# Attention and gated projection on one core: transposes, tail scores and attention outputs share PSUM bank pairs by quarters, the gated tile is stored without padding, and the step order is written anew

## The chip, the cores and the metric

The kernel runs on one core of a Trainium2 chip. The metric is the device time of one execution in microseconds.

## The reference: what is computed

q, k and v are 8 batches x 8 heads x 576 rows x 64. Attention is causal by blocks of 64 rows. Its output, with the heads side by side, is the input x of a gated linear unit of width 512: a causal convolution over five rows gives the gate, x times w_val gives the value, and their product goes through w_out.

```
scores = scale * np.matmul(q, k.transpose(0, 1, 3, 2))
mask = block_i >= block_j                      # blocks of 64
attn = softmax(where(mask, scores, -1e9))
x = (attn @ v) with heads side by side         # 8 x 576 x 512
gate = 1 / (1 + np.exp(-gate_pre))             # gate_pre: conv of 5 taps over rows
out = gate * (x @ w_val) @ w_out               # 8 x 576 x 512, float32
```

## The kernel before, in words

**Work units.** A head pair p (0 to 31; batch p // 4) is the unit of attention on the first 512 rows of a batch. The last 64 rows of a batch (the tail) are handled for all eight heads together. The gated unit works on a ring of four batch slots, each 4 + 576 columns wide (`slot(b)`, line 219), cut into runs n of 464 columns (0 to 9, five to a ring, `RUN`).

**Steps.** The kernel has no loops over these units. The string PLAN (line 12) lists 987 steps as name/arguments/engine/banks, in the order in which they are emitted; each engine executes its own steps in that order, and semaphores tie the engines together. Engine letters are P (TensorE), V (VectorE, DVE in the profile), A (ScalarE, ACT), G (GpSimd, POOL) and S (the SP DMA queue). The steps used below:

- `lq`, `lk`, `lv`, `lt`, `lvt`, `lwv`, `lwo`, `lcv`: loads of q, k, v, the tails of q and k, the tail of v, w_val, w_out, the convolution weights. q and k land in five buffers, v in five, tails in two (lines 193 to 196).
- `cq`, `cv`, `ct`, `cvt`: casts to fp16. `ccv`, `cwv`, `cwo`: casts of the weights.
- `T` (16 transposes), `Te`: q and k of a pair transposed into a pair of PSUM banks, and the copy out. `TT`, `TTe`: the same for a batch's tails.
- `S/p.t` (t = 0, 1, 2), `E/p.t`: scores of 128 x 1024, and their exponentials on ACT (line 441). `SL`, `EL`: scores of the tail with itself.
- `mka`, `mkb`: zeros into the masked corners. `A` (20 matmuls of 65 columns), `N`: attention times v, and the division by the row sum (lines 490 and 491). `AT`, `NT` for the tail.
- `X`, `Xe` (line 229 or 231), `XT`, `XTe`: transposes into the ring `xt`.
- `C/n` (80 matmuls on 32 x 32 tiles), `CS/n.i`: convolution of a run into four banks, and tanh on ACT (line 598).
- `V/n.x` (4 matmuls of 464 columns), `Ve/n.x`: x times w_val, and gate times value into `gv` (line 613).
- `W`, `We`: w_out reordered. `O/u.t` (4 matmuls of 512 columns, 8 where t = 4), `Oe`, `Od`: 128 output rows of the batch pair u, copy out, store. `OL` is one half of the very last rows.

**PSUM.** There are eight banks. A step that writes two banks has the pair to itself from its first write until its copy-out has run: `where` (line 173) records the banks, `take` (line 175) hands them to the copy-out. The loop at the end (lines 667 to 690) frees steps on other banks from each other:

```
for x, at in held:
    if not at & mine:
        independent(i, x, overwrite)
```

so that what stays tied is what shares a bank: a writer waits for the copies out of its banks, and a copy-out waits for the latest writer of its banks. `T` uses half of each bank of its pair (2 x 512 fp16 values), `TT` and `X` a quarter (2 x 256 fp16), `SL` half (2 x 256 fp32), `A` 260 of 512 fp32 values.

**The gated tile.** `gv` has the ring's layout, with four unused columns per batch. A run of 464 columns is one `Ve`. `project` (line 618) takes 128 columns of `gv` at a time; the fifth block (t = 4) lies across two batches, so that it takes two groups of 64 columns and eight matmuls.

Of the kernel before, what the change touches and what calls it, by code (L numbers as in the profile page):

```python
# [12 lines left out]
lk/1/S ppool//G pdve//V lcv//S ccv//G CW//P/1 lq/1/A cq/1/V T/1/P/4+5 lq/0/S lk/0/S lt/0.1/S  # L13
lt/0.0/S ct/0/G lk/4/S lq/3/S CWe//V lk/3/S cq/3/G cq0/0/V T0/0/P/0+1 lq/2/S lk/2/S lq/4/S cq0/1/V
T0/1/P/2+3 Te/1/A pact//A S/1.1/P/4+5 lv/1.0/S lv/0.0/S lv/0.1/S S/1.0/P/6+7 lt/1.0/S lq/5/S
lv/2.1/S T0e/0/V lk/5/S T0e/1/A S/0.0/P/2+3 lv/1.1/S lv/2.0/S lvt/0/S lv/3.1/S lt/1.1/S TT/0/P/0+1
lk/6/S TTe/0/V lv/3.0/S lq/6/S cq/4/G E/1.1/A E/0.0/A lwv/1/S lwv/0/S SL/0/P/0+1 EL/0/A S/0.2/P/2+3
E/1.0/A S/1.2/P/4+5 E/1.2/A S/0.1/P/0+1 T/3/P/6+7 cq/2/V T/2/P/4+5 mka/1/G cv/0/G Te/3/A S/3.1/P/6+7
E/0.1/A T/4/P/0+1 Te/2/V S/2.2/P/4+5 lwo/1/S lwo/0/S E/0.2/A mka/0/G mkb/0/G lk/7/S S/2.1/P/2+3
lq/7/S lt/2.0/S Te/4/V S/4.0/P/0+1 E/3.1/A E/2.2/A E/2.1/A S/2.0/P/6+7 E/2.0/A A/0/P/4+5 S/3.2/P/6+7  # L20
cq/5/V T/5/P/2+3 lt/2.1/S lk/8/S lv/4.1/S lq/10/S E/4.0/A N/0/V cv/2/V X/0/P/4+5 mkb/1/G cv/1/G
A/1/P/0+1 lq/8/S Xe/0/V E/3.2/A S/4.1/P/4+5 N/1/V S/3.0/P/6+7 mkb/3/G mkb/2/G mka/2/G Te/5/A
S/5.0/P/2+3 lk/10/S E/4.1/A ct/1/G cv/3/G lv/4.0/S A/2/P/0+1 N/2/V lq/9/S lk/9/S lv/6.0/S E/3.0/A
mka/3/G S/5.1/P/4+5 E/5.1/A TT/1/P/6+7 TTe/1/V lv/5.1/S cvt/0/G cq/6/G A/3/P/0+1 N/3/V cwv/1/G
cwo/0/G E/5.0/A ct/2/G lv/7.1/S S/4.2/P/6+7 SL/1/P/4+5 lv/6.1/S EL/1/A mka/4/G cq/7/G E/4.2/A
mkb/4/G cq/8/G lq/13/S lv/5.0/S lv/7.0/S lvt/1/S lk/12/S lq/12/S lk/11/S lq/11/S AT/0/P/2 X/1/P/4+5
X/3/P/0+1 Xe/3/A T/6/P/6+7 Te/6/A X/2/P/0+1 Xe/2/A NT/0/V XT/0/P/3 S/6.0/P/6+7 E/6.0/A Xe/1/V
C/0/P/0+1+4+5 CS/0.1/A CS/0.0/A XTe/0/V cwv/0/V V/0.3/P/7 cwo/1/V Ve/0.3/V V/0.0/P/6 Ve/0.0/V
S/6.1/P/4+5 E/6.1/A W//P/0+1+2+3 We/0/A We/1/V S/5.2/P/6+7 TT/2/P/4+5 TTe/2/V V/0.2/P/2 SL/2/P/0+1
S/6.2/P/4+5 E/5.2/A T/7/P/6+7 Ve/0.2/V Te/7/V EL/2/A E/6.2/A V/0.1/P/0 S/7.0/P/4+5 mka/6/G E/7.0/A  # L30
S/7.1/P/2+3 T/8/P/6+7 Te/8/A E/7.1/A Ve/0.1/V O/0.0/P/4 Oe/0.0/V mkb/6/G S/8.1/P/6+7 E/8.1/A cq/10/G
T/10/P/0+1 Te/10/V S/7.2/P/4+5 cv/4/G A/4/P/2+3 S/8.0/P/6+7 N/4/V E/7.2/A E/8.0/A O/0.1/P/1 cq/9/G
cv/6/G T/9/P/2+3 Te/9/V O/0.2/P/0 Oe/0.2/V cv/7/G mka/7/G Oe/0.1/A mkb/7/G mkb/5/G mka/8/G
S/8.2/P/6+7 E/8.2/A A/6/P/4+5 N/6/V S/10.2/P/2+3 S/9.1/P/0+1 X/6/P/4+5 cv/5/V cvt/1/G mkb/8/G
mka/5/G lv/8.0/S lv/8.1/S E/9.1/A S/9.2/P/6+7 Xe/6/A A/7/P/0+1 lt/3.1/S lt/3.0/S E/9.2/A N/7/V
AT/1/P/5 E/10.2/A A/5/P/6+7 NT/1/V cq/12/G T/12/P/0+1 XT/1/P/5 X/7/P/2+3 N/5/V X/5/P/6+7 lq/14/S
lk/13/S lv/9.0/S lt/4.0/S lk/14/S lv/9.1/S lk/15/S lv/11.0/S lt/4.1/S lv/10.1/S XTe/1/V lq/15/S
cq/11/G lv/10.0/S lv/11.1/S lvt/2/S lv/12.1/S cv/8/G lv/13.1/S ct/3/G lv/12.0/S lk/16/S cq/13/G
lk/18/S Xe/7/V lq/18/S lq/16/S mkb/9/G w0/1.64.0/P/4 X/4/P/4+5 Te/12/A S/12.1/P/2+3 cq/14/G cv/9/G
lv/14.0/S lv/14.1/S Xe/5/A T/11/P/6+7 E/12.1/A Xe/4/V C/1/P/0+1+4+5 CS/1.1/A V/1.2/P/2 Te/11/V  # L40
CS/1.0/A S/10.1/P/6+7 Ve/1.2/V A/8/P/4+5 N/8/V E/10.1/A S/11.0/P/2+3 V/1.1/P/0 E/11.0/A S/10.0/P/4+5
# [70 lines left out]
def kernel(  # L112
# [44 lines left out]
    def one(b):  # L157
        return PS[0:128, b]
# [562 lines left out]
```

## Time and profile before

| what | us |
| --- | --- |
| median of three runs | 185.79 (185.62 to 188.61) |
| the profiled execution, its own time | 187.27 |
| its span, first to last instruction | 185.0 |
| PE busy | 162.9 (88%) |
| ACT busy | 144.3 (78%) |
| DVE busy | 115.5 (62%) |
| POOL busy | 81.6 (44%) |

The profile page gives busy time of each engine, a strip of 40 slices of the span, DMA queues, the chain of work that ended last, and groups of equal instructions. Other views used here are the timeline (instructions in order, with start and length; equal neighbours merged), the windows (busy time in chosen stretches) and the waits. A line number can be that of a helper: 136 is every matmul, 140 every transpose on TensorE, 229 and 231 every copy.

### The profile page before, as it was taken

To read this page: it belongs to the slowest core of one execution; us is meant where nothing else is said; L and a number is where in the kernel's file an instruction comes from. 1 tells how busy PE (TensorE), PEld (TensorE's weight loads), DVE (VectorE), ACT (ScalarE), POOL (GpSimd) and SP (SyncE) were. 2 spreads that over 40 slices of the span, in tenths; PEclk is the share of its full clock that TensorE was granted. 3 is DMA by queue.
4 is the path that set the end of the run, shared out by engine and by line. 5 is a ranking of instruction groups with operands and counts; after the bars stand their busy time and mean duration, and the time that the engine had idled before them with its cause. 6 is when DMAs were issued, how large, how long until landed. Compare 5 with 4: busy or idle time off the path is not lost.

```text
span 185.0 us, 8265 instructions
## 1 busy us (share of the span) xinstructions
PE 162.9 (88%) x3529; PEld 98.6 (53%) x3529; DVE 115.5 (62%) x218; ACT 144.3 (78%) x170; POOL 81.6 (44%) x197
## 2 busy tenths in 40 slices
PE   0658787779869999999999998999999999999992
PEld 0333574345754566756446564566556655665450
DVE  6725565758666887696486885578458765533730
ACT  2599999788868998989998879997796888362342
POOL 6226362564854787625550771862843306200000
PEclk9999999999999999999999999999999999999998
DMA  5896999987988899699598999994896634104076
GB/s 177 269 273 144 237 292 370 273 231 172 288 204 217 200 268 278 148 343 311 147 259 243 265 275 283 283 245 129 226 272 203 149 141 164 66 4 174 0 275 235
DMA packets 66494, 40.38 MB, mean 218 GB/s; under 512 B 40214, under 2 KB 60950, under 8 KB 66459
## 3 DMA queue, kind: packets, MB, share of 16 engines
q1 hardware_dynamic: 66042, 39.48, 75.3%
q8 instruction: 27, 0.44, 1.0%
q10 hardware_dynamic: 416, 0.39, 0.7%
q14 instruction: 9, 0.07, 0.1%
HBM read 30.42 MB, written 9.44 MB: 215 GB/s over the span
## 4 chain that ended last, share of the span: by engine, by line
PE 65%; DMA 11%; ACT 9%; DVE 6%; issue 3%; SPq 3%; POOL 1%; DVEq 0%; ACTq 0%; POOLq 0%
PE PS L136 59%; ACT pt L441 6%; DMA qks<-in_k_dram 6%; PE PS L140 5%; DMA qks<-in_q_dram 4%; DVE x L491 2%; DVE qkT L231 2%; SPq L243 2%; DMA vs<-in_v_dram 2%; ACT xt L229 1%; DVE gv L613 1%; DVE osb L231 1%; ACT osb L229 1%; POOL qk L231 1%; ACT qkT L229 1%
## 5 line engine op out<-in xcount | busy, mean ns | idle before, releaser
L441 ACT ACTIVATE pt<-PS 128x1024 f16<-128x1024 f32 x96 | 93.4, 1030 | 10.3 <-PE PS L136 8.4
L136 PE MATMUL PS<-xt,w_val 128*128 128x464 f16 x160 | 36.9, 360 | 0.3 <-ACT pt L456 0.2
L136 PE MATMUL PS<-qkT 64*128 64x256 f16 (+3 forms) x256 | 34.2, 319 | 2.5 <-ACT qkT L229 0.5
L136 PE MATMUL PS<-w_out,gv 128*128 128x512 f16 (+2 forms) x164 | 36.0, 376 | 0.2 <-DMA qks<-in_q_dram 0.2
L231 POOL CAST qk<-qks 128x1024 f16<-128x1024 f32 x28 | 29.1, 1042 | 15.2 <-DMA qks<-in_q_dram 4.1
L613 DVE SCALAR_TENSOR_TENSOR gv<-th,PS 128x464 f16<-128x464 f32 x40 | 24.8, 634 | 16.5 <-PE PS L136 10.0
L136 PE MATMUL PS<-v,pt 128*128 128x65 f16 (+1 forms) x896 | 31.5, 195 | 1.1 <-DVE x L491 0.3
L136 PEld LDWEIGHTS <-pt 128*128 128x128 f16 (+1 forms) x960 | 28.3, 103 | 6.9 <-issue 3.3
L136 PEld LDWEIGHTS <-qkT 64*128 64x128 f16 x512 | 16.7, 97 | 18.8 <-issue 11.8
L231 DVE COPY qkT<-PS 128x1024 f16<-128x1024 f16 (+1 forms) x19 | 22.6, 1192 | 3.6 <-PE PS L140 3.4
L598 ACT ACTIVATE th<-PS 128x928 f32<-128x928 f32 x20 | 17.8, 946 | 7.8 <-PE PS L136 7.7
L491 DVE TENSOR_TENSOR x<-PS,rc 128x512 f16<-128x512 f32 x32 | 22.1, 691 | 1.1
L231 POOL CAST v<-vs 128x512 f16<-128x512 f32 x30 | 18.3, 620 | 8.1 <-DMA vs<-in_v_dram 7.5
L136 PEld LDWEIGHTS <-w_val 128*128 128x128 f16 x160 | 13.8, 97 | 14.1 <-issue 2.6
L136 PEld LDWEIGHTS <-gv 128*128 128x128 f16 (+1 forms) x164 | 12.9, 100 | 12.9 <-issue 2.0
L140 PE MATMUL PS<-ident,qk 64*128 64x64 f16 x512 | 14.2, 198 | 5.2 <-DVE qk L231 2.9
L229 ACT COPY qkT<-PS 128x1024 f16<-128x1024 f16 (+1 forms) x14 | 13.8, 985 | 5.6 <-PE PS L140 5.5
L231 DVE COPY xt<-PS 128x512 f16<-128x512 f16 (+1 forms) x32 | 12.3, 391 | 8.8 <-PE PS L140 8.6
L463 POOL MEMSET pt<- 64x256 f16 x32 | 9.8, 306 | 16.8 <-ACT pt L441 15.9
L469 POOL MEMSET pt<- 64x128 f16 x32 | 6.2, 199 | 24.6 <-ACT pt L441 23.9
L231 DVE COPY osb<-PS 128x512 f32<-128x512 f32 x17 | 11.5, 688 | 8.1 <-PE PS L136 6.4
L140 PEld LDWEIGHTS <-qk 64*128 64x128 f16 x512 | 11.2, 99 | 10.0 <-issue 4.1
(62 smaller groups left out, 138.7 us busy)
## 6 DMA issues: line engine op xcount, KB each, us to landing
out_dram<-osb SPq DMA_DIRECT2D x35, 256.0 KB, 2.9
qks<-in_k_dram SPq DMA_DIRECT2D x32, 256.0 KB, 4.1
vs<-in_v_dram SPq DMA_DIRECT2D x64, 128.0 KB, 4.3
qks<-in_q_dram SPq DMA_DIRECT2D x31, 256.0 KB, 4.2
tls<-in_k_dram SPq DMA_DIRECT2D x16, 64.0 KB, 3.8
tls<-in_q_dram SPq DMA_DIRECT2D x16, 64.0 KB, 3.8
vts<-in_v_dram SPq DMA_DIRECT2D x8, 128.0 KB, 4.6
gv<-in_moe_w_val_dram SPq DMA_DIRECT2D x2, 512.0 KB, 6.3
```

What stands on the lines that cost most here:

```text
L136: made.append(nc.tensor.matmul(out=out, lhsT=lhsT, rhs=rhs, start=start, stop=stop, skip_group_check=True))
L140: made.append(nc.tensor.transpose(out=out, in_=in_, identity=identity))
L229: i = nc.scalar.copy(out=out, in_=in_)
L231: i = (nc.vector if eng == "V" else nc.gpsimd).tensor_copy(out=out, in_=in_)
L243: DMA[eng].dma_start(out=rot(qks, p)[0:128, i], in_=(q, k)[i][b, 2 * g:2 * g + 2, 0:512, 0:64].rearrange("h (p n) d -> p h (n d)", n=4))
L441: made.append(nc.scalar.activation(out=rot(pts, p)[0:128, 0:2, 512 * t:512 * t + 512], in_=both(take("S", p, t)), func=AF.Exp, bias=0.0, s ...
L463: nc.gpsimd.memset(pt[64:128, 0:2, 0:1024].rearrange("p h (t s) -> p h t s", t=2)[:, :, :, 0:64], 0.0)
L469: nc.gpsimd.memset(rot(pts, p)[64:128, 0:2, 1024:1088], 0.0)
L491: made.append(nc.vector.tensor_tensor(out=rot(x16, p)[0:128].rearrange("p i h d -> p h i d"), in0=r[:, :, :, 0:64], in1=rc[0:128].to_broad ...
L598: made.append(nc.scalar.activation(out=rot(ths, n)[0:128, 2 * i:2 * i + 2], in_=both(take("C", n, i))[:, :, 0:RUN], func=AF.Tanh, bias=0.0 ...
L613: made.append(nc.vector.scalar_tensor_tensor(out=gv[0:128, x, o:o + RUN], in0=rot(ths, n)[0:128, x], scalar=1.0, in1=one(take("V", n, x))[ ...
```

## The change

1. `place` and `placed` are new. A tile takes quarters of a bank pair: `T` and `SL` take quarters 0+1 or 2+3, `TT` and `X` one quarter (3, 2, 0 or 1, the first that is free), `A` quarters 0 to 2. Tiles with disjoint quarters may be in the same pair at once. `S`, `AT`, `XT`, `V`, `O`, `C` keep banks for themselves.
2. `gv` has 4 x 576 columns without padding. `Ve` writes each piece of a run that lies in one batch with an instruction of its own: runs with n % 5 of 1, 2 or 3 have two pieces, the others one, 64 instructions instead of 40. `project` takes 128 columns in every block, four matmuls also for t = 4.
3. PLAN has 989 steps in a new order, with other banks and some steps on other engines. By kind the same steps remain, with three `w0` (one 512-column matmul on zeros each) instead of one: two among the first 100 steps on PE in place of one that ran at 52 us, and one as the very last step. Copies on DVE instead of ACT: `Oe` 22 (17 before), `Te` 21 (18), `Xe` 26 (25), `TTe` 7 (6); `XTe` on DVE 4 (7). `lk/0` instead of `lq/1` goes over ACT's DMA queue. The last two runs change places: `C/9` comes ahead of `C/8`.

```diff
+    spots = {}
+    PAIRS, SINGLES = ((0, 1), (2, 3)), ((3,), (2,), (0,), (1,))
+
+    def place(banks, choices, *key):
+        used = {z for b, zs in spots.values() if b == tuple(banks) for z in zs}
+        zs = next(c for c in choices if not used & set(c))
+        spots[key], where[key] = (tuple(banks), zs), banks
+        return 256 * zs[0]
+
+    def placed(*key):
+        banks, zs = spots.pop(key)
+        return take(*key), 256 * zs[0]
...
-    gv = const([128, 4 * RING], fp16, "gv")
+    gv = const([128, 16 * SEQ], fp16, "gv")
...
     def T(p, eng, bank):
-        where["T", p] = bank
+        o = place(bank, PAIRS, "T", p)
         for i in range(2):
-            transposes(rot(qk16, p), i, both16(bank))
+            transposes(rot(qk16, p), i, both16(bank), o)
...
     def SL(b, eng, bank):
-        where["SL", b] = bank
+        o = place(bank, PAIRS, "SL", b) // 2
...
     def A(p, eng, bank):
-        where["A", p] = bank
+        place(bank, ((0, 1, 2),), "A", p)
...
     def X(p, eng, bank):
-        where["X", p] = bank
+        o = place(bank, SINGLES, "X", p)
         for i in range(4):
-            halves(both16(bank), 64 * i, rot(x16, p)[0:128, i, 0:2, 0:64])
+            halves(both16(bank), o + 64 * i, rot(x16, p)[0:128, i, 0:2, 0:64])
...
     def Ve(n, x, eng, bank=None):
-        o = RUN * (n % 5)
-        made.append(nc.vector.scalar_tensor_tensor(
-            out=gv[0:128, x, o:o + RUN], in0=rot(ths, n)[0:128, x], scalar=1.0,
-            in1=one(take("V", n, x))[:, 0:RUN], op0=ALU.add, op1=ALU.mult))
+        o, r = RUN * (n % 5), one(take("V", n, x))
+        for i in range(4):
+            a, e = max(o, slot(i)), min(o + RUN, slot(i) + SEQ)
+            if a < e:
+                made.append(nc.vector.scalar_tensor_tensor(
+                    out=gv[0:128, x, a - 4 * i:e - 4 * i], in0=rot(ths, n)[0:128, x, a - o:e - o],
+                    scalar=1.0, in1=r[:, a - o:e - o], op0=ALU.add, op1=ALU.mult))
...
     def project(u, t, r, a, e):
-        o = slot(2 * u) + 128 * t + (4 if t > 4 else 0)
+        o = SEQ * (2 * u % 4) + 128 * t
         for fc in range(4):
-            for m, c, k in ((0, o, 64), (64, o + 68, 64)) if t == 4 else ((0, o, 128),):
-                mm(r[m:m + k, 0:e - a], gv[0:128, fc, c:c + k], w_out_sb[0:128, fc, a:e],
-                   start=(fc == 0), stop=(fc == 3))
+            mm(r[:, 0:e - a], gv[0:128, fc, o:o + 128], w_out_sb[0:128, fc, a:e],
+               start=(fc == 0), stop=(fc == 3))
```

The new order around the weights, the first convolution and the first output (words of PLAN, other words left out):

```
... w0/1.64.1/P/7 ... lwo/0/S lq/7/S ... lk/7/S ... lwv/0/S ... lwv/1/S ... lwo/1/S ...
... cwv/0/V C/0/P/2+3+6+7 ... S/8.2/P/4+5 S/7.1/P/0+1 ... S/7.0/P/6+7 ... cwv/1/V V/0.2/P/2 ...
... W//P/2+3+6+7 ... O/0.0/P/4 ... T/10/P/2+3 O/0.1/P/5 ... T/9/P/0+1 ... X/7 ... XT/1 ... C/1 ...
```

More of the change, by code (lines that the diff above doesn't have):

```diff
@@ L12 @@
 PLAN = """
[L13 to L17, printed above, removed]
@@ L24 @@
[L24 to L29, printed above, removed]
@@ new lines @@
+lv/1.1/S TT/1/P/2+3 TTe/1/V cq/6/G T/3/P/0+1 E/1.2/A lv/1.0/S mka/2/G ct/2/G SL/1/P/0+1 EL/1/A
+mkb/2/G S/4.0/P/2+3 lwo/0/S lq/7/S E/4.0/A S/4.2/P/6+7 Te/3/V S/3.1/P/0+1 E/3.1/A mkb/0/G mkb/1/G
+S/3.0/P/4+5 E/3.0/A cv/3/G cv/0/G T/6/P/2+3 cq/5/V T/5/P/2+3 S/3.2/P/0+1 E/3.2/A lk/7/S mka/3/G
+E/4.2/A w0/1.64.0/P/4 lwv/0/S Te/6/V S/6.1/P/4+5 Te/5/V mkb/3/G cq/8/G lwv/1/S TT/2/P/0+1
+S/4.1/P/2+3 E/4.1/A S/5.1/P/6+7 TTe/2/V lwo/1/S cv/1/G cvt/0/G A/0/P/0+1 N/0/V E/6.1/A E/5.1/A
+A/3/P/2+3 cq/7/G lq/12/S X/0/P/2+3 lv/4.1/S lv/4.0/S lk/12/S lq/10/S lk/10/S lt/3.1/S lk/9/S lq/9/S
@@ new lines @@
+S/5.2/P/4+5 E/5.2/A T/8/P/0+1 cv/2/V A/2/P/6+7 lv/6.1/S lt/3.0/S lv/6.0/S Te/8/A N/3/V X/3/P/4+5
+N/2/V lv/5.0/S lv/5.1/S lv/7.0/S lv/7.1/S SL/2/P/4+5 Xe/0/A S/5.0/P/0+1 E/5.0/A S/8.0/P/6+7 lvt/1/S
+X/2/P/2+3 A/1/P/2+3 Xe/3/V E/8.0/A N/1/V Xe/2/V AT/0/P/0 NT/0/V EL/2/A S/8.1/P/6+7 E/8.1/A
+S/6.2/P/1+2 E/6.2/A S/6.0/P/4+5 X/1/P/6+7 E/6.0/A XT/0/P/3 XTe/0/V Xe/1/V T/7/P/0+1 Te/7/A cwv/0/V
+C/0/P/2+3+6+7 CS/0.1/A S/8.2/P/4+5 S/7.1/P/0+1 mka/5/G mka/6/G mka/8/G CS/0.0/A cwo/1/G S/7.0/P/6+7
+mkb/4/G mkb/5/G cwv/1/V V/0.2/P/2 Ve/0.2/V V/0.1/P/3 Ve/0.1/V cwo/0/G E/7.1/A cv/4/G E/7.0/A mka/4/G
@@ new lines @@
+mkb/8/G S/10.2/P/6+7 NT/1/V E/10.2/A XT/1/P/1 Xe/5/V C/1/P/2+3+4+5 XTe/1/A CS/1.1/A CS/1.0/A
+T/11/P/0+1 lv/8.0/S lv/11.0/S lv/10.0/S lv/9.0/S lv/9.1/S TT/3/P/0+1 lv/10.1/S TTe/3/A lv/11.1/S
+lk/15/S Te/11/V O/0.2/P/7 Oe/0.2/V V/1.1/P/5 Ve/1.1/V S/9.0/P/2+3 lq/15/S S/11.2/P/6+7 E/11.2/A
+lvt/2/S V/1.3/P/0 Ve/1.3/V V/1.0/P/1 Ve/1.0/V cq/13/G E/9.0/A mkb/10/G S/11.0/P/4+5 E/11.0/A
+T/13/P/6+7 SL/3/P/6+7 Te/13/V EL/3/A cq/14/G T/14/P/2+3 V/1.2/P/0 Ve/1.2/V Te/14/A mkb/11/G mkb/9/G
+ct/4/G S/11.1/P/4+5 E/11.1/A TT/4/P/6+7 lk/16/S cv/8/G mka/9/G A/8/P/6+7 mka/10/G S/13.0/P/2+3
@@ new lines @@
+cv/14/G A/14/P/0+1 N/14/V V/2.2/P/4 cq/19/G S/17.0/P/6+7 E/17.0/A X/14/P/0+1 Ve/2.2/V X/15/P/0+1
+T/19/P/0+1 Te/19/V lk/20/S lt/6.0/S lv/17.1/S lt/5.1/S S/17.2/P/2+3 E/17.2/A S/18.2/P/4+5 cvt/3/G
+AT/3/P/6 lt/5.0/S Od/0.2/S lv/17.0/S E/18.2/A S/19.1/P/2+3 lt/6.1/S V/2.3/P/7 NT/3/V XT/3/P/6
+cq/21/G T/21/P/4+5 E/19.1/A Xe/14/V Xe/15/V XTe/3/V lv/16.0/S lv/16.1/S S/19.2/P/0+1 V/2.0/P/6
+E/19.2/A lk/23/S lq/23/S mka/17/G mka/18/G S/19.0/P/2+3 cq/20/G E/19.0/A lq/22/S Te/21/V Ve/2.0/V
+Ve/2.3/V lk/22/S C/3/P/0+1+4+5 CS/3.0/A lk/24/S lq/24/S C/4/P/2+3+6+7 V/3.1/P/0 Ve/3.1/V O/0.8/P/1
@@ new lines @@
+V/4.2/P/3 Oe/0.7/V Ve/4.2/V mka/19/G Od/0.5/S lv/21.1/S E/20.1/A mka/16/G lk/26/S E/21.0/A O/1.0/P/1
+Te/23/A A/16/P/6+7 lv/22.0/S lk/27/S S/21.1/P/4+5 mkb/19/G cvt/4/G mka/20/G S/24.0/P/2+3 lq/27/S
+cv/19/G N/16/V V/4.1/P/0 lvt/5/S lt/7.1/S cq/25/G Od/0.7/S mkb/21/G T/22/P/6+7 lv/22.1/S Oe/1.0/V
+E/24.0/A Od/0.8/S X/16/P/6+7 lv/23.0/S lt/7.0/S lv/23.1/S lq/29/S Od/0.4/S Ve/4.1/V X/18/P/6+7
+Xe/18/V Xe/16/V E/21.1/A mka/21/G lq/28/S lk/28/S AT/4/P/1 S/24.1/P/2+3 cv/20/G lv/25.0/S NT/4/V
+mkb/20/G T/25/P/4+5 Te/22/A Te/25/V V/3.0/P/0 XT/4/P/1 XTe/4/V E/24.1/A Ve/3.0/V S/22.1/P/6+7
@@ new lines @@
+Xe/22/V T/28/P/6+7 Te/28/V S/27.1/P/0+1 E/27.1/A O/1.6/P/5 Oe/1.6/V XT/5/P/2 X/25/P/3+4 T/31/P/3+4
+Te/31/V XTe/5/A S/29.2/P/6+7 E/29.2/A S/28.0/P/0+1 V/5.0/P/2 V/5.2/P/5 Xe/25/V E/28.0/A S/26.2/P/6+7
+C/6/P/0+1+3+4 E/26.2/A CS/6.1/A Ve/5.0/V Ve/5.2/V lv/30.0/S O/2.1/P/2 cv/24/G A/24/P/6+7 mkb/27/G
+CS/6.0/A O/2.2/P/3 lvt/7/S cv/26/G lv/31.1/S mkb/26/G N/24/V lv/29.1/S mka/26/G A/26/P/0+1 lv/28.0/S
+X/24/P/0+1 N/26/V S/28.2/P/6+7 S/28.1/P/4+5 Xe/24/V Oe/2.1/A E/28.1/A E/28.2/A V/6.3/P/2 Ve/6.3/V
@@ L410, in TTe @@
     def TTe(b, eng, bank=None):
+        bank, o = placed("TT", b)
         copy(eng, ktails[b % 2][0:128].rearrange("p g i s -> p (g i) s")[:, :, 0:64].rearrange(
             "p g (r s n) -> p r g n s", r=2, n=2),
-             both16(take("TT", b))[:, :, 0:256].rearrange(
+             both16(bank)[:, :, o:o + 256].rearrange(
                  "p r (g n s) -> p r g n s", g=8, n=2))
@@ L451, in SL @@
                 hp = slice(64 * h, 64 * h + 64)
[L452 removed]
+                mm(both(bank)[:, h, o + 64 * g:o + 64 * g + 64], kt[hp, g, 1, 0:128], kt[hp, g, 0, 0:64])
     @op
     def EL(b, eng, bank=None):
+        bank, o = placed("SL", b)
         made.append(nc.scalar.activation(
             out=pt4[b % 2][0:128, 0:8].rearrange("p (h g) s -> p h (g s)", h=2),
[L458 removed]
+            in_=both(bank)[:, :, o // 2:o // 2 + 256], func=AF.Exp, bias=0.0, scale=0.125))
     @op
@@ L487, in N @@
     def N(p, eng, bank=None):
-        r = both(take("A", p))[:, :, 0:260].rearrange("p h (i d) -> p h i d", d=65)
+        r = both(placed("A", p)[0])[:, :, 0:260].rearrange("p h (i d) -> p h i d", d=65)
         rc = rot(rcs, p)
@@ L544, in Xe @@
         b, g = divmod(p, 4)
+        bank, o = placed("X", p)
         copy(eng, xt[0:128, g, slot(b) + 4:slot(b) + 516].rearrange("p (i r s) -> p i r s", i=4, r=2),
-             both16(take("X", p))[:, :, 0:256].rearrange("p r (i s) -> p i r s", i=4))
+             both16(bank)[:, :, o:o + 256].rearrange("p r (i s) -> p i r s", i=4))
     @op
```

157 lines of the change are left out of this document (66 added, 91 removed).

## The prediction

> **What bounds the kernel now.** I read the page's strip first, then the windows of five stages, then the timeline for what one step costs TensorE (PE). The strip:
>
> ```profile
> PE   0658787779869999999999998999999999999992
> DMA  5896999987988899699598999994896634104076
> ```
>
> PE is full from about slice 12 (55 us) to the end; ahead of that it is not, and there the DMA engines are nearly full. The windows are cut at C/0 (30.2 us), C/1 (54.8), C/2 (76.4), at 150 and at the end of the last matmul; columns are length, then PE, PEld, DVE, ACT, POOL, clock, DMA share, GB/s.
>
> ```profile
> 0.00:30.20 30.20, 17.99 (x391) 12.09 (x392) 17.42 (x38) 23.78 (x28) 13.71 (x47) 1.00 0.87 243
> 30.20:54.80 24.60, 20.08 (x486) 12.49 (x485) 15.52 (x26) 20.29 (x23) 13.81 (x28) 1.00 0.90 243
> 54.80:76.40 21.60, 21.09 (x507) 13.14 (x505) 16.63 (x29) 19.33 (x22) 15.35 (x34) 1.00 0.90 233
> 76.40:150.00 73.60, 72.46 (x1646) 43.80 (x1646) 50.80 (x96) 64.09 (x73) 34.38 (x76) 1.00 0.85 236
> 150.00:182.20 32.20, 31.28 (x532) 17.11 (x528) 15.15 (x32) 16.80 (x24) 4.30 (x13) 1.00 0.36 131
> ```
>
> To 30 us ACT is the fullest engine (23.8 of the 24 us since its first copy at 6.5). From 54.8 on PE is. So a change pays after 54.8 if it takes work off PE, and before that if loads and ACT bring C/1 on sooner.
>
> What a step costs PE is the distance between its start and the next one's. From the timeline:
>
> ```profile
> 170.07 3.31 PE L136 MATMUL PS<-xt,w_val 128*128 128x464 f16 x16
> 173.21 8.06 PE L136 MATMUL PS<-w_out,gv 128*128 128x512 f16 x44
> ...
> 61.17 0.96 PE L136 MATMUL PS<-xt,w_val 128*128 128x464 f16 x4
> 62.06 0.39 PE L136 MATMUL PS<-qkT 64*128 64x512 f16 x2
> ...
> 18.37 1.28 PE L136 MATMUL PS<-v,pt 128*128 128x65 f16 x20
> 19.82 0.28 PE L136 MATMUL PS<-qkT 64*128 64x256 f16 x2 [0.17 <-ACT pt L441]
> ...
> 21.71 0.78 PE L136 MATMUL PS<-v,pt 128*128 128x65 f16 x20
> 22.43 0.82 PE L136 MATMUL PS<-qkT 64*128 64x384 f16 x8
> ```
>
> Four V steps in a row take 3.14 us, 0.785 each. One V followed by an S takes 0.89. The 0.10 more is the price of going from full-height matmuls (128 rows) to half-height ones (64 rows). It appears the same way on A (0.61 followed by A or V, 0.71 by S), O (0.864 by its like, 0.967 by others) and S (0.22 by S or T, 0.32 by A, V or O). The last four lines show that PE ran at half speed early: the first A took 1.45 less 0.17 idle, the second 0.72.
>
> So PE's work is: S 96 x 0.22 = 21.1, V 40 x 0.787 = 31.5, O 31 x 0.864 + 4 x 0.885 + two halves = 31.2, A 32 x 0.608 = 19.5, AT 5.3, C 11.5, T 7.4, X 3.8, small steps 3.7, together 135.0; and 157 places in PE's order where the tile shape changes, 15.7. Sum 150.7. The span is 5.3 (to the first matmul) + 150.7 + 26.2 (stalls and half speed) + 2.8 (last copy and store). By stage, with PE's work before C/1 29.7 and before C/2 49.2, the 26.2 are 19.8 to C/1, 2.1 to C/2, 4.2 after (0.1 is rounding).
>
> **The change part by part.** The sum is made against the profiled execution: span 185.0, its own time 187.27, so 2.27 lies around the span. It ran 1.48 above the median of 185.79; I take the difference from the median.
>
> *Shape changes.* The new PE order has 130 instead of 157, counted the same way: 27 x 0.10 = -2.7. Bounds: -2.9, and -1.4 if the half of them ahead of C/1 lies in time that PE waits anyway.
>
> *Four matmuls for t = 4.* PE's group of gv matmuls loses 16, which at the group's 376 ns would be 6.0 us. But the two 64-column groups run beside each other: O/0.4 took 0.987 against 0.967 of other O steps. So 4 x 0.02 = -0.1; bounds 0 and -0.1.
>
> *Two more w0.* Two early ones in place of one at 52 us, +0.2 at most (that one took 0.07, an S of as many columns 0.22), I take 0.1; the last one runs beside the last store (2.9 us), nothing; if it were on the path, 0.2.
>
> *24 more Ve pieces.* One Ve of 464 columns takes 634 ns, the copy of 256 columns 425, a reciprocal of 8 columns 205. A line through the first two has 0.16 at zero columns, of which 0.08 overlap with the next. So 24 x 0.08 to 0.16 = 1.9 to 3.8 us of DVE. With five more Oe (0.61 each), three more Te (1.14) and the rest, DVE's work goes from 111 to 120 us of step time, under PE's 148; ACT's falls from 137 to 132. I cost this at nothing: PE's work covers it. If the cover is gone, up to 3.8 for the pieces. At the very end V/8.1 is followed by O/3.0 and OL/1 (1.3 us), which cover its two pieces (0.8) and leave the last O chain without a gap, as before.
>
> *Sharing of pairs.* A copy-out waits for the latest writer of its banks, so with a neighbour in the pair it waits for that too, and the next full user waits for both copies. In the new order 33 copies have such a neighbour; in 29 of them it is PE's next step, in four the next but one, so the copy starts 0.1 to 0.7 us later. After the first 12 us of PE work, 32 reuses of a pair follow two or three copies, and by PE's work in between they have room: all but five have slack left after the copies (0.1 to 2.7 us). In both orders I counted reuses of a bank with less than 0.5 us to spare: 109 before, 84 in the new one. Cost: nothing taken; bounds -2 (half of the 4.2 of late stalls go) and +8 (33 x 0.25).
>
> The Trainium skill (PSUM — Partial Sum Buffer, section PSUM bank collisions raise a hardware error) speaks against the idea: engines have to be kept apart by bank and 32-partition quadrant, not by address, so quarters of a bank give room and no independence. By that rule every one of the 33 would be tied as I have it, and the sum would be between the same -4.0 and the slower rival below; no run here shows an access of two engines to one bank.
>
> *Order up to C/1.* C/1 needs batch 1 complete. Before, p = 0 to 8, 9, 10, 11, 12 were transposed ahead of it (cq/11 ended the last wait, T/11 at 53.2 to 54.6 us); now 11 is not, it follows C/1. Three things bound it. ACT: 41.1 us of work stand ahead of C/1 in both orders, from 6.5 at the earliest 47.6, with the 1.2 us that ACT idled to 31 us in the trace 48.8. PE: 28.4 of work (29.7 before). Loads: the last weight load, lwo/0, landed at 32.05 with 7.5 MB behind it, 234 GB/s. In the new order lvt/1, the last load that batch 1 needs, is issued with 11.8 MB: 50.4 us. Then cvt 0.6, AT 0.76 and NT, XT, XTe 1.3 in part beside each other: C/1 at 52.4. Loads end last, so stalls to C/1 are 52.4 - 5.3 - 28.4 = 18.7 against 19.8: -1.1. Bounds: 48.8 (ACT alone): -4.7; and loads at the 213 GB/s that the smaller ones ahead of the weights had (5.1 MB by lv/3.0's landing at 24.05 us): 55.4, C/1 at 57.4: +5.0.
> Queue by queue: SP issues q and k of nine pairs ahead of lwv/1 and lwo/1 (before, of seven), so these land by the same rate near 36 and 37. cwv/1 holds V/0.2 until about 36.7, when PE (C/0 at 33.5 by ACT's 26.1 of work, then 2 us) would be free at 35.5: a stall of 1.2, in the 18.7. What stands behind it on PE is A/4 and O/0.0; ACT has three E and two tanh to do meanwhile, so it doesn't run dry. ccv moves from POOL (599 ns) to DVE ahead of cq/1, about 0.4 there, and lk/1 is third instead of first on SP; T/1 slips from 5.8 to about 6.1 and the first E from 8.36 to 8.3 to 8.5: nothing. SL/0's copy waits for T/2 (its neighbour), which loads let go at about 10.8, when ACT gets to it at 12.9: nothing.
>
> *After C/1.* To C/2, PE 20.5, ACT 20.8, DVE 17.8 (before 19.5, 18.8, 15.8): ACT is as full as PE here. C/3 and C/4 stand back to back on all eight banks; four tanh of 0.93 let the next S in 0.4 us late. Against that stand the easier bank reuses. I take the stalls of 2.1 + 4.2 as 6.1: -0.2. Bounds -2 and +4.
>
> Sum: -2.7 - 0.1 + 0.1 - 1.1 - 0.2 = **-4.0**. That is 183.3 for an execution like the profiled one, and 185.8 - 4.0 = **181.8** against the median.
>
> **The rivals.** (1) *ACT alone sets the start*, loads keep up: C/1 at 48.8 gives 3.6 more, 178.2. For it: ACT's 23.8 of 24 us. Against it: DMA share 0.87 to 0.90. (2) *Loads set it, at the slower rate.* Weights behind two more pairs land after 38 us, C/1 comes between 54.5 and 57.4: 183.9 to 186.8, about no change. For it: the DMA line, and waits for q, k and v loads in the first 42 us of the chain that ended last. (3) *Slower: a shared pair is one lock.* PE executes in order, so if a neighbour's copy holds up the pair's next user, all steps behind stand. The 33 shared pairs need a second copy of 0.42 (Xe) to 1.22 us (Te). Break-even against -4.0 is at 0.12 us each; at 0.23 each the kernel is slower by 2%, and at 0.42, the full price of an Xe, it takes 195.7. For it: DVE, which does most of these copies, goes to 17.8 of 20.5 us between C/1 and C/2. Against it: the slack above. (4) *The sharing itself does little* and the new order the rest. 37 of 317 PE steps find a neighbour in their pair; this changes no number of the forecast.
>
> **How the numbers follow.** Forecast 0.55, own range 179.5 to 184; 182.1 (2%) lies just above its middle, so 0.33 of it is faster, 0.22 within. Rival 1 0.10, faster. Rival 2 0.20, within but for 0.01 slower. Rival 3 0.15, slower. Together faster 0.43, same 0.41, slower 0.16; 2% is about what a measurement of this kernel can tell from no change. The range goes from 178.2 (rival 1) to 189.0, which leaves out some 0.05 below and 0.15 above.
>
> **What would show it.** In the changed profile: C/1 near 52 us and C/2 near 74.5; V x4 followed by S still 0.89; O with t = 4 at 0.86 or 0.97; from C/2 to the last matmul about 103 us (105.8 before). If copies of shared pairs were the price, the waits view would name line 229 or 231 ahead of PE after 55 us, with more than the 1.7 us of idle PE of now. Wrong would be the forecast if C/1 comes after 56 us, or if the stalls after C/2 pass 8 us.

## The result, and the profile after

The changed kernel takes 194.94 us (median of four runs, 193.50 to 195.32) against 185.70 us (184.52 to 188.61) for the kernel before: 1.051 times as long, interval 1.042 to 1.059. The forecast was 181.8, its range 178.2 to 189.0. It was slower by some 9 us where a gain of 4 was forecast. Ratios, here and below, are to the kernel before and leave out executions more than 1.5% above the fastest of the same kernel. The profiled execution took 195.19 us, its span 193.2.

The strip of the changed kernel:

```profile
PE   0568697799878889979998999979899799999992
DMA  6898999987998699766999999997520450322266
```

PE's row still has 7s and 8s after slice 12, with single slices short of full to slice 32. The DMA row, to the left, is as full as before.

The windows, cut at the same steps as before (C/0, C/1, C/2, at 150 us, and behind the last matmul), with the same columns:

```profile
0.00:36.30 36.30, 23.34 (x470) 16.12 (x470) 23.31 (x46) 26.67 (x31) 15.18 (x49) 1.00 0.93 266
36.30:55.30 19.00, 15.93 (x391) 10.20 (x385) 11.11 (x21) 16.04 (x20) 13.72 (x26) 1.00 0.88 239
55.30:83.30 28.00, 23.89 (x532) 15.38 (x532) 17.07 (x36) 22.27 (x26) 15.77 (x37) 0.94 0.85 222
83.30:150.00 66.70, 62.92 (x1496) 39.17 (x1495) 47.29 (x96) 54.84 (x62) 31.75 (x69) 1.00 0.76 209
150.00:190.40 40.40, 38.41 (x636) 21.21 (x635) 23.33 (x53) 19.17 (x28) 5.56 (x17) 1.00 0.38 136
```

C/0 comes at 36.3 instead of 30.2. C/1 comes at 55.3, only 0.5 later than before. From C/1 to C/2 it takes 28.0 us instead of 21.6, and PE is idle for 4.1 of them (before 0.5). No engine is full there: ACT has 22.3 of 28.0 us, DVE 17.1. So the engines wait for each other.

PE's waits in the changed kernel (line waited for, total, times, longest):

```profile
PE PS L136 <- DVE conv L245: 5.0, 1, 5.0
PE PS L136 <- DVE qkT L245: 4.2, 5, 1.3
PE PS L136 <- ACT pt L457: 2.4, 6, 1.1
PE PS L136 <- ACT th L616: 2.3, 3, 1.4
PE PS L140 <- DVE qk L245: 2.2, 2, 1.5
PE PS L136 <- DVE x L508: 1.8, 4, 0.9
PE PS L136 <- DVE xt L245: 1.6, 1, 1.6
PE PS L140 <- DVE x L508: 1.3, 1, 1.3
```

The first is the start, which was there before (5.3). The copies of the transposes (qkT, 4.2) had 0.5, 0.5 and 0.2 on three lines before. Those for N (x, line 508) are 3.1 in place of 1.6; those for tanh (th) and for Xe (xt) are new. A view of waits shows the last link only; behind it stands a queue of copies. Here is that queue at C/2, from the timeline (start, length, engine, line, operation, and in brackets the idle time before it and what ended it):

```profile
80.03 0.41 PE L140 MATMUL PS<-ident,qk 64*128 64x64 f16 x16
80.42 0.29 PE L140 MATMUL PS<-ident,x 64*128 64x64 f16 x8
...
81.46 1.02 ACT L243 COPY qkT<-PS 128x1024 f16<-128x1024 f16 x1
...
82.51 1.09 DVE L245 COPY xt<-PS 128x512 f16<-128x512 f16 x3 [2.15 <-ACT qkT L243]
83.32 1.27 PE L136 MATMUL PS<-xt,DG 32*32 32x464 f16 x80 [1.58 <-DVE xt L245]
```

T/18 and the X steps 10 and 12 lie in quarters of one pair (banks 0 and 1). The X were done by 80.71. DVE was free and could have copied them out. But T/18's copy stands ahead of theirs in PLAN and belongs to ACT. ACT had three E to do first and came to it at 81.46, and DVE stood idle for 2.15 us until that copy ended at 82.48. Then come Xe/10, Xe/13 and Xe/12 in a row; the convolution, which needs the banks that Xe/13 empties (4 and 5), waits for that copy, and PE with it for 1.58 us. Nothing in this chain is long. It is one engine's queue that is handed over to another through a pair of banks.

So it is in the whole trace. In 33 steps PE writes into a pair that still holds one or two other tiles, which makes 37 places where two tiles share a pair. Of these, 20 have their copies on different engines, and no two of these copies overlap; the one that PLAN names first always runs first. In 14 of the 20 the second copy starts within 0.1 us of the end of the first. The longest idle time that such a copy ended is 4.79 us of DVE, ahead of Te/11, by TTe/3 on ACT.

### The profile page after: what moved, and what is told of

It is laid out like the page before. It is cut to its first block, busy times and chain, and to the rows that moved or that the text cites. A ratio compares the mean times of both kernels' runs of the same rounds, so it can differ in the third digit from the quotient of the medians.

```text
span 193.2 us, 8216 instructions
## 1 busy us (share of the span) xinstructions
PE 164.5 (85%) x3515; PEld 102.1 (53%) x3515; DVE 122.1 (63%) x249; ACT 139.0 (72%) x164; POOL 82.0 (42%) x196
## 4 chain that ended last, share of the span: by engine, by line
PE 53%; ACT 17%; DVE 12%; issue 6%; DMA 6%; SPq 2%; POOL 2%; ACTq 0%; DVEq 0%; POOLq 0%
PE PS L136 49%; ACT pt L457 8%; PE PS L140 5%; DVE qkT L245 5%; DMA qks<-in_k_dram 4%; ACT th L616 4%; DMA qks<-in_q_dram 2%; DVE x L508 2%; ACT qkT L243 2%; ACT pt L473 2%; DVE gv L634 1%; POOL v L245 1%; ACT xt L243 1%; DVE kt L245 1%; DVE rc L507 1%
## 5 line engine op out<-in xcount | busy, mean ns | idle before, releaser
L457 ACT ACTIVATE pt<-PS 128x1024 f16<-128x1024 f32 x96 | 93.3, 1029 | 15.3 <-PE PS L136 14.3
L136 PE MATMUL PS<-qkT 64*128 64x512 f16 (+3 forms) x256 | 34.6, 328 | 7.6 <-DVE qkT L245 4.2
L634 DVE SCALAR_TENSOR_TENSOR gv<-th,PS 128x112 f16<-128x112 f32 (+5 forms) x64 | 26.3, 449 | 18.1 <-PE PS L136 12.6
L136 PE MATMUL PS<-w_out,gv 128*128 128x512 f16 (+1 forms) x148 | 35.9, 376 | 1.4 <-DVE x L508 1.4
L245 DVE COPY qkT<-PS 128x1024 f16<-128x1024 f16 (+1 forms) x23 | 26.9, 1175 | 15.8 <-PE PS L140 7.5
L245 POOL CAST qk<-qks 128x1024 f16<-128x1024 f32 x27 | 27.9, 1046 | 5.7 <-DMA qks<-in_k_dram 2.6
L136 PEld LDWEIGHTS <-qkT 64*128 64x128 f16 x512 | 18.4, 100 | 20.9 <-issue 10.3
L480 POOL MEMSET pt<- 64x256 f16 x32 | 10.7, 335 | 33.7 <-ACT pt L457 33.0
L616 ACT ACTIVATE th<-PS 128x928 f32<-128x928 f32 x20 | 17.8, 947 | 9.4 <-PE PS L136 9.3
L136 PEld LDWEIGHTS <-w_val 128*128 128x128 f16 x160 | 13.9, 97 | 16.6 <-issue 5.1
L136 PEld LDWEIGHTS <-gv 128*128 128x128 f16 x148 | 13.1, 98 | 15.1 <-issue 1.8
L245 DVE COPY osb<-PS 128x512 f32<-128x512 f32 x22 | 14.9, 685 | 5.8 <-PE PS L136 5.3
L140 PE MATMUL PS<-ident,qk 64*128 64x64 f16 x512 | 14.3, 202 | 2.5 <-DVE qk L245 2.2
L243 ACT COPY qkT<-PS 128x1024 f16<-128x1024 f16 x10 | 10.2, 1018 | 7.3 <-PE PS L140 5.5
L136 PE MATMUL PS<-xt,DG 32*32 32x464 f16 x800 | 13.7, 380 | 1.7 <-DVE xt L245 1.6
```

The source lines that it names most:

```text
L136: made.append(nc.tensor.matmul(out=out, lhsT=lhsT, rhs=rhs, start=start, stop=stop, skip_group_check=True))
L140: made.append(nc.tensor.transpose(out=out, in_=in_, identity=identity))
L243: i = nc.scalar.copy(out=out, in_=in_)
L245: i = (nc.vector if eng == "V" else nc.gpsimd).tensor_copy(out=out, in_=in_)
L457: made.append(nc.scalar.activation(out=rot(pts, p)[0:128, 0:2, 512 * t:512 * t + 512], in_=both(take("S", p, t)), func=AF.Exp, bias=0.0, s ...
L480: nc.gpsimd.memset(pt[64:128, 0:2, 0:1024].rearrange("p h (t s) -> p h t s", t=2)[:, :, :, 0:64], 0.0)
```

## The experiments

For the account I use what a stage takes beyond PE's work in it, by the durations of steps that the prediction had worked out (so: idle PE, and PE at half speed or a lower clock). The time up to PE's first work is left out. Experiment e3, the old order in the new code, is the reference, as its profiled execution (184.75) is at its median. The last two columns are e9 and e10, told below.

| beyond PE's work, us | e3, old order | changed kernel | e9: new order, hardly shared | e10: old order, same steps left out |
| --- | --- | --- | --- | --- |
| to C/0 | 12.4 | 17.7 | 16.1 | 12.4 |
| C/0 to C/1 | 5.0 | 4.1 | 6.5 | 8.0 |
| C/1 to C/2 | 2.1 | 7.5 | 3.8 | 3.4 |
| C/2 to C/5 | 2.3 | 2.0 | 2.0 | 1.6 |
| C/5 to C/7 | 1.2 | 4.8 | 2.9 | 1.6 |

From C/7 on nothing is lost in any of them (30.5 us in the changed kernel up to the end of its last O, for some 31 us of work). By the same durations PE's work is 148 us in the changed kernel, some 2 less than in e3.

My theory after seeing the trace: tiles that share a pair are coupled, copy to copy and copy to writer, and that is the price. Rivals: it is two engines reading one pair, and would go if one engine did both copies; the code (more Ve pieces) costs; the new order by itself is worse, or its late start is.

**e1: the new order without sharing across engines.** Banks were handed out anew, the longest free first (222 words of PLAN differ).

```diff
-CW//P/3 ... T/1/P/0+1 ... T/2/P/2+3 ... Te/23/A
+CW//P/7 ... T/1/P/4+5 ... T/2/P/6+7 ... Te/23/V
```

> The changed kernel, same steps in the same order, but with banks given out anew so that almost no pair is shared: 8 shares are left, all between copies of one engine (one copy, Te/23, goes from ACT to DVE for that); the changed kernel has 37 shares, 20 of them between a copy on ACT and a copy on DVE. Lock theory (two copies out of one pair on two engines run one after the other, and the engine that waits holds up its whole queue): the PE waits behind such copies after 50 us (8.8 us in the changed kernel's trace, plus about 1.5 us at half speed after one of them) mostly go, so 186 to 189 us. Order theory (the new order itself starts the convolution 6 us later and has the queues too full): 193 to 195 us.

Measured: 225.89 (225.08 to 226.86), ratio 1.224 (1.216 to 1.231). Neither theory had this. Its waits of PE:

```profile
PE PS L133 <- ACT pt L454: 11.6, 19, 2.0
PE PS L137 <- ACT pt L454: 5.9, 10, 1.1
```

Line 454 is E. Of these 17.5 us of waiting, 15.3 stand ahead of steps that do not read the exponentials, so what they waited for is the pair that the exponential had to empty. At eleven steps the new order has more tiles alive than eight banks hold unless some share. So this order can't be tried without its shares by new banks alone, and e1 says nothing about the price of a share.

**e2: both copies of a shared pair on one engine.** 18 copies move to their neighbour's engine.

```diff
-Te/18/A ... Te/26/A ... Xe/6/A ... TTe/3/A ... Te/13/V
+Te/18/V ... Te/26/V ... Xe/6/V ... TTe/3/V ... Te/13/A
```

> The changed kernel with its banks and all its shares, but 18 copies moved to the engine of their neighbour in the pair, so that no pair is read by two engines. Lock theory by readers on two engines: 187 to 190 us, the idle time of DVE and ACT that ended with the other engine's copy (Te/11 4.8 us, Xe/10 2.2, Te/26 1.5, Te/30 1.4, N/7 1.4) is gone. If a copy's wait for its neighbour's write is what costs, or the order: 193 to 196 us, since the shares are all still there and DVE has more to do.

Measured: 194.30 (193.74 to 194.89), ratio 1.052 (1.047 to 1.058), the same as the changed kernel. C/1 to C/2 took 26.0 instead of 28.0, C/4 to C/5 26.8 instead of 25.1. The wait for the other engine becomes a place in the same engine's queue: taking the change of engines away saves nothing.

**e3: the old order in the new code.** PLAN of before, everything else changed.

> The order, banks and engines of before in the changed code: no pair is shared, the gated tile is unpadded (64 Ve pieces instead of 40, four matmuls for t = 4). All theories: 185 to 187 us; the pieces cost DVE 2 to 4 us beside PE. A rival that lays the loss on the pieces or on the unpadded tile: 190 us or more.

Measured: 184.68 (ten runs, 183.80 to 185.35), ratio 0.999 (0.996 to 1.003). The 64 pieces of Ve, the unpadded `gv` and the four matmuls for t = 4 cost nothing. All of the loss is in PLAN. The window from C/1 to C/2 in e3:

```profile
52.50:74.00 21.50, 21.00 (x495) 13.00 (x489) 16.82 (x33) 19.98 (x23) 13.93 (x32) 1.00 0.89 223
```

DVE had 16.8 us of work here and ACT 20.0, in 21.5 us. In the changed kernel they had 17.1 and 22.3, in 28.0.

**e4: the old order, with shares put in.** 16 T, X, TT and SL go into the pair of a neighbour one to three steps ahead, whose copy is on the other engine.

```diff
-X/0/P/4+5 T/7/P/6+7 T/18/P/6+7 SL/6/P/2+3 T/31/P/2+3
+X/0/P/2+3 T/7/P/0+1 T/18/P/4+5 SL/6/P/0+1 T/31/P/6+7
```

> The order of before in the changed code, with the second bank pair of 16 steps replaced by the pair of a step one to three places ahead, each time one whose copy runs on the other engine. Nothing else is moved. Lock theory: 189 to 194 us, new PE waits behind DVE or ACT copies that follow the other engine's. Order theory: as with the order of before, 185 to 187 us.

Measured: 202.22 (201.19 to 203.07), ratio 1.095 (1.088 to 1.102), more than either theory had: 17.5 us over e3 for 16 shares, 1.1 each. One of them, SL/6 beside T/25, in the timeline of e4:

```profile
123.94 0.29 PE L132 MATMUL PS<-kt 64*128 64x64 f16 x8
124.40 0.60 ACT L469 ACTIVATE pt<-PS 128x512 f16<-128x512 f32 x1
125.04 1.23 DVE L241 COPY qkT<-PS 128x1024 f16<-128x1024 f16 x1 [2.22 <-ACT pt L469]
126.18 0.68 DVE L241 COPY osb<-PS 128x512 f32<-128x512 f32 x1
126.32 0.61 PE L132 MATMUL PS<-qkT 64*128 64x512 f16 x2 [2.09 <-DVE qkT L241]
```

DVE waits 2.22 us until ACT has done EL/6, copies T/25, and PE stands 2.09 us for S/25.0, which needs it. The shares were not chosen with an eye on room, so 1.1 is dear; and a moved tile also takes its pair at another time, which this run does not separate.

**e5: the same 16 shares, copies on one engine.** As e4, with 14 copies moved to their neighbour's engine.

```diff
-Te/18/V ... Te/25/V ... Xe/28/V ... TTe/5/A
+Te/18/A ... Te/25/A ... Xe/28/A ... TTe/5/V
```

> The order of before with the same 16 shared pairs as the run before this with the order of before, which took 202.2 us, but with one copy of each group moved to its neighbour's engine (one group keeps two engines). If the price of sharing is that two engines can't read a pair at once: 185 to 190 us. If it is that a copy-out waits for the neighbour's write and the pair's next user for both copies, whatever the engine: 196 to 203 us.

Measured: 204.66 (203.63 to 207.08), ratio 1.106 (1.100 to 1.112), not less than e4. Eleven of the 14 copies went on to ACT, which is the fuller engine, and that may hide a gain here; in e2 eight went to ACT and ten to DVE. Neither run shows the gain that the rival of two engines asks for: the coupling costs on one engine as well.

**e6, e7, e8: is it the start?** In the changed kernel the load of k of pair 1 is third on SP's queue, T/1 starts at 6.79 instead of 5.82, and PE's steps take twice their time until about 26 us (before to 19.5). Two runs put matmuls on zeros early in PE's order, one gives the first loads the old order.

```diff
+w0/9.128.0/P/7
```

(e6: in the changed kernel, ahead of PE's first step)

> The changed kernel with nine more matmuls on zeros (512 columns, full height) as PE's first work, while it waits for the first loads. If the late start of the convolution (36.3 us against 30.2 before) comes from PE at half speed (10 us of its steps' time beyond their full-speed cost to C/0, against 6.6 before): C/0 2 to 4 us sooner and 191 to 193 us. If ACT and the loads set the start: 194 to 196 us.

```diff
+w0/9.128.0/P/7 ... w0/3.128.0/P/6 ... w0/4.128.0/P/4
```

(e7: in the old order, at the start, ahead of T/3 and ahead of T/2)

> The order of before in the changed code, with nine such matmuls as PE's first work and seven more in the two waits of PE at 12 and 13 us. Half-speed theory: 182 to 184 us, C/0 one to two us sooner. Loads and ACT set the start: 184.5 to 186 us. Against it speaks that the extra matmuls can hold up the steps behind them: up to 188.

```diff
-lq/1/S lcv//S ... lk/1/S ... lk/0/A ... lq/0/S
+lk/1/S lq/1/A lcv//S lq/0/S lk/0/S
```

(e8: in the changed kernel)

> The changed kernel with its first loads on the queues and in the sequence of before: k of pair 1 first on SP, q of pair 1 on ACT's queue, k of pair 0 on SP after q of pair 0. The first copy on ACT came at 7.4 us instead of 6.5. If ACT's late start is handed down to the end: 193.5 to 194.5 us, one us less. If later waits absorb it: as the changed kernel, 194.9.

Measured: e6 195.04 (193.81 to 196.63), ratio 1.056 (1.048 to 1.064), no gain, though C/0 came some 1.6 us sooner in the profiled execution. But in that execution the granted clock was 0.67 from 10 to 20 us and 0.58 from 20 to 30, against 1.00 in the changed kernel's and in e7's, which has the fillers too. So e6 does not show what a start at full speed would be worth. e7 189.93 (188.50 to 190.41), ratio 1.025 (1.018 to 1.032), above its range: the fillers themselves hold up T/2 (16.2 us instead of 13.3), and C/2 comes 6.3 us later than in e3. e8 194.16 (193.12 to 198.26), ratio 1.049 (1.043 to 1.055): C/0 comes 1.0 sooner and the gain is handed down to the end, where it is 0.8; the granted clock was 1.00 throughout in e8's profile, 0.988 in the changed kernel's, so dips of the clock are not the cause either. What the first loads are worth is about 1 us of the loss; what half speed is worth, none of the three runs shows.

**e9 and e10: take the sharing out, in both orders.** The small member of all but three shared groups is not computed in PSUM; its copy reads a tile in SBUF of the same size instead, so that part of the output is not computed. e10 leaves the same 30 steps out of the old order, where they share nothing, so that it shows what the missing work is worth.

```diff
-X/10/P/0+1 X/12/P/0+1 ... Xe/10/V ... Xe/12/V ... TT/3/P/0+1 ... TTe/3/A
+Xs/10/V ... Xs/12/V ... Ts/3/A
```

> The changed kernel without sharing, at its own order and banks: of each shared pair but three the small member is left out of PSUM (23 X, 3 TT, 4 SL of pairs, whose PE work isn't done; their copies read as many elements of the step's input in SBUF instead, on the same engine at the same place; part of the output is so not the reference's). The next run leaves the same steps out of the order of before; the two are to be compared. Coupling theory (what costs is that tiles in one pair wait for each other): this one within 2 us of the next or below it, some 176 to 181 us. Order theory: 5 to 9 us above the next one, 186 to 190 us.

> The order of before in the changed code with the same 23 X, 3 TT and 4 SL left out of PSUM as in the run before this (their copies read the input in SBUF; part of the output is so not the reference's). It shares nothing, so only the work left out counts: about 3.5 us of PE and some shape changes less, 178 to 182 us by all theories.

Measured: e9 185.46 (ten runs, 182.78 to 189.82), ratio 0.993 (0.989 to 0.998); e10 183.15 (ten runs, 181.69 to 185.81), ratio 0.989 (0.985 to 0.993). Both are longer than I had expected. The ratios rest on five runs of e9 and eight of e10, 182.78 to 184.93 and 181.69 to 184.41; the profiled executions took 186.89 and 185.45, so the two columns of the table above are about 3 us too high in all. By the ratios, taking the shares out brings the new order down by 0.057 (1.051 less 0.993), 10.6 us; it brings the old order, which had none, down by 0.010 (0.999 less 0.989), 1.9 us. So the coupling is 0.047, 8.7 us; with the four intervals added in squares, between 6.7 and 10.7. By the medians of all runs, instead of the ratios, it is about 8. What the new order costs without it is the difference of e9 and e10, 0.004, 0.8 us, and that is within the intervals of no difference (2.3 by the medians of all runs).

The control has a limit: in the new order the steps left out may also save something at waits that have nothing to do with a share, and e10 can't show that. Seen from PE, its idle time after 50 us (pauses of 0.15 us and more) is 9.9 us in the changed kernel, 4.8 in e9 and 2.2 in the kernel before. Of e9's 4.8, 1.44 stand behind Te/27 and Te/26, one of the three groups that were left in, as they do in the changed kernel; so e9 is not quite free of shares. The window from C/1 to C/2 in e9:

```profile
55.30:78.70 23.40, 21.38 (x472) 13.62 (x472) 17.81 (x36) 21.17 (x26) 14.47 (x33) 1.00 0.97 259
```

C/1 is where it was in the changed kernel; C/2 comes 4.6 us sooner, of which 1.0 is work left out.

**e11: the sharing out only between C/1 and C/2.** The steps X 8 to 12, TT 3 and 4 and SL 3.

```diff
-SL/3/P/6+7 ... TT/4/P/6+7 ... X/9/P/0+1 ... X/10/P/0+1 X/12/P/0+1
+Ls/3/A ... Ts/4/V ... Xs/9/V ... Xs/10/V ... Xs/12/V
```

> The changed kernel with only the small members of the shared pairs between C/1 and C/2 left out of PSUM in that manner (X 8 to 12, TT 3 and 4, SL 3; part of the output is so not the reference's). C/1 to C/2 took 28.1 us there against 21.6 before. Coupling theory: 22 to 24 us for that stage, and 190 to 191.5 us in all. Order theory: the stage stays at 26 us or more, 193 to 195 us.

Measured: 193.84 (191.30 to 196.18), ratio 1.038 (1.027 to 1.049). The stage did what the coupling says, 23.7 us instead of 28.0, of which 1.0 is work left out. The end didn't: of the 5.5 us that C/2 came sooner, 1.0 was left at C/5 in the profiled execution. There PE stopped in the middle of C/4:

```profile
91.19 0.90 PE L132 MATMUL PS<-xt,DG 32*32 32x464 f16 x48
94.70 0.42 PE L132 MATMUL PS<-xt,DG 32*32 32x464 f16 x16 [2.61 <-issue]
95.06 1.57 PE L132 MATMUL PS<-xt,w_val 128*128 128x464 f16 x4
```

Nothing that the profile shows releases it after 2.61 us, and the next V takes 1.57 us instead of 0.79; from C/2 to C/5 it takes 42.8 us instead of 38.3. So the effect of this stage alone on the whole time is not settled: its fastest run, 191.3, lies in the range that I had for the coupling, its median does not.

## Why the prediction was wrong

**Right: what the shapes, t = 4 and the pieces cost.** PE's work of 148 us is counted with the same durations as in the sum, but they hold where I looked: from C/7 on, and in single steps. A V followed by steps of the other shape still takes 0.89 and an O with a different neighbour 0.96:

```profile
105.65 1.03 PE L136 MATMUL PS<-w_out,gv 128*128 128x512 f16 x4
106.61 0.61 PE L136 MATMUL PS<-qkT 64*128 64x384 f16 x6
...
110.59 0.96 PE L136 MATMUL PS<-xt,w_val 128*128 128x464 f16 x4
111.48 0.41 PE L140 MATMUL PS<-ident,qk 64*128 64x64 f16 x16
```

The O at 105.65 took 0.96 to the next step, the V at 110.59 0.89. The Ve group went from 24.8 to 26.3 us of DVE, 1.5 for 24 more pieces (estimated 1.9 to 3.8), and e3 shows that the cover held. The end came without a gap: the last `w0` (189.10 to 189.48) is over before the last copy (189.31 to 189.90).

**Wrong: "Sharing of pairs. Cost: nothing taken".** This is the step that failed. It measured 8.7 us (e9 against the changed kernel, less e10 against e3), a little more than the bound of 8 that I had kept for it (33 x 0.25). I had counted room by PE's work alone: so many steps of PE lie between a tile's write and the next use of its pair, and the copies fit into that. But the copies do not start when their tile is written. They stand in the queues of ACT and DVE, which have 22 and 17 us of other work in that stage, and a shared copy waits for its neighbour's copy as well, which my count did not have: I had the next writer wait for both copies, and a copy wait for the neighbour's write. In the trace the copies of a pair on two engines never run together. The account of PSUM that I gave ahead of the change lacks this tie too. The Trainium skill (PSUM — Partial Sum Buffer, section PSUM bank collisions raise a hardware error) says that a compiler's scheduler puts a dependency between any two instructions on different engines that touch one bank and 32-partition quadrant, reads as well as writes; the 20 pairs of copies agree with that. I had read the section for the write, and not for the two reads.

What takes time is then not the second copy but the waiting for the other engine's turn: 2.15 us of idle DVE for 1.02 us of copy at C/2. Where the queue behind it is PE's, PE stops too. In the changed kernel, eight such chains that I followed back through a shared pair after 50 us cost PE 7.4 of its 9.9 us of idle time (1.27, 0.63, 0.57, 0.47, 1.58, 0.53, 1.44, 0.91).

**Wrong, by less: the order.** Without the sharing the new order is no gain (e9 and e10 0.4% apart), in spite of 2 us less work for PE. C/0 was forecast at 33.5 and came at 36.3; of the 2.8 us, e8's first loads give back 1.0, and e9 has C/0 at 34.1. Against e3's 29.4 the later C/0 was in the forecast, and was to be made good by C/1. It was, mostly: the stage from C/0 to C/1 was 19.0 us instead of 23.1 in e3, yet C/1 came at 55.3 and not at 52.4. The reason is not the one that I had bounded. Loads were faster than I took them: `lvt/1` landed at 47.5 (forecast 50.4) and `lwo/1` at 34.8 (37). The last wait ahead of C/1 was of X/7, 1.27 us for N/7, which had waited 1.39 us for Xe/6 on ACT, its neighbour in the pair:

```profile
52.75 0.61 ACT L243 COPY xt<-PS 128x512 f16<-128x512 f16 x1
...
53.39 0.21 DVE L507 RECIPROCAL rc<-PS 128x8 f32<-128x8 f32 x1 [1.39 <-ACT xt L243]
53.63 0.69 DVE L508 TENSOR_TENSOR x<-PS,rc 128x512 f16<-128x512 f32 x1
...
54.38 0.29 PE L140 MATMUL PS<-ident,x 64*128 64x64 f16 x8 [1.27 <-DVE x L508]
```

**The stalls after C/1** were taken as 6.1 and were 14.3 (7.5, 2.0 and 4.8 in the table). My sign for that was set at the wrong place, after C/2, where they were 6.8; most of them lay ahead of it. The other sign, copies ahead of PE after 55 us, came true: 2.5 us of waits on the lines of copies, 8.4 us of idle PE in all.

**The rivals.** It is the third, the shared pair as one lock, to which I gave 0.15. Its break-even was 0.12 us for each of 33 pairs, and the runs show 8.7 / 33 = 0.26. That its figure of 195.7 lies near the measured time is chance in part: it had 13.9 us for the locks and none lost in the order. The evidence that I set against it, the slack, was the count that failed. Evidence for it stood beside it, DVE with 17.8 of 20.5 us between C/1 and C/2, and in the part on the time after C/1, ACT as full as PE there: copies have a queue ahead of them. The second rival has C/1 in its interval (54.5 to 57.4), but the loads were not what ended last. The first falls with C/1 at 55.3 instead of 48.8. The evidence for it was read too high: of ACT's 23.8 us, 1.3 lie ahead of its first copy, so that it was busy for 22.5 of the 23.8 us that follow. The fourth falls with e4 and e9; the steps that find a neighbour are 33, not 37.

**Slips of the sum that change nothing.** The upper bound of the order up to C/1, +5.0, is counted from C/1 at 52.4; counted from the 19.8 us of the kernel before, as the lower bound is, it is +3.9. The cut at 182.2 us lies 0.9 behind the last matmul (181.3) and 0.3 behind the last copy, so the 2.8 us at the end are the store alone, and the 26.2 us of stalls hold the 0.9.

The account, against e3 by the ratios (1.051 less 0.999, 9.5 us): PE's work -2, the coupling +8.7, which leaves about +3 for the order beyond PE's work, by the table most of it up to C/0. The last is a remainder, and as uncertain as the coupling's interval.

## What to carry to other kernels

Count a shared buffer by who empties it, not by who fills it: the slack of a tile ends when the queue of the engine that copies it gets there, and with a neighbour in the same bank it is the later of two queues. By these traces I would put one more tile into a bank only where both copies are next in their queues; no run here shows a share that pays. Where an order is packed to need more room than there is, test the sharing in the old order (e4) and its absence in the new one (e9, with e10 as its control); new banks alone (e1) only move the shortage.

## What was not expected of the hardware

- PE stood for 2.61 us in e11, 1.20 in e9 and 1.04 in the kernel before, in the middle of a run of equal matmuls, with no releaser in the profile. In e11, PE's steps then took twice their time for some 5 us, with a granted clock of 0.66:

```profile
92.00:94.70 2.70, 0.09 (x12) 0.00 (x0) 0.00 (x0) 0.90 (x2) 0.00 (x0) 1.00 1.04 333
95.00:100.00 5.00, 5.00 (x48) 2.01 (x34) 1.48 (x4) 2.90 (x4) 0.04 (x1) 0.66 1.11 277
```

DVE and POOL did nothing either in the first of these windows, while the DMA engines were full (1.04). What held the engines stays open.

- Matmuls on zeros at the start (e6) did not do away with the stretch in which PE's steps take twice their time. The nine ran from 1.2 to 5.0 us, and the 16 transposes of T/1 behind them took 0.41 us instead of 0.61. From 10 to 30 us the granted clock in that execution was 0.67 and then 0.58, and PE's other steps lost some 9 us up to C/0, against 10.1 without them. With the 1.8 us that the nine took beyond 0.22 each it is 11.0.
